# Attention, mixing and gated-MLP kernel on one core: the spatial product of three batches as seven half products

## Chip, cores and metric

The kernel runs on one core of a Trainium2 chip. The metric is the device time of one execution in microseconds (us). The times of before are 612.1, 614.9 and 610.61 us, median 612.1.

## The reference

Three models follow one another on B = 4 batches of S = 768 tokens with d = 384 features (8 heads of 48). First linear attention with a decayed state, then token mixing with a rotation by theta and a channel layer, then a gated MLP with a spatial product. Everything is float32.

```python
def _attn_ref(q, k, v, alpha):
    for t in range(S):
        state = alpha[:, :, t, :, None] * state + np.einsum('bhd,bhe->bhde', k[:, :, t], v[:, :, t])
        y[:, :, t] = np.einsum('bhd,bhde->bhe', q[:, :, t], state)

def _moe_ref(x, w_theta, w_tok_r, w_tok_i, w_ch):
    theta = x @ w_theta
    y = np.einsum('ts,bsd->btd', w_tok_r, x * cos(theta)) + np.einsum('ts,bsd->btd', w_tok_i, x * sin(theta))
    u = x + y
    return u + np.maximum(u @ w_ch, 0.0)

def _moe2_ref(x, w_in, w_spatial, b_spatial, w_out):
    h = np.maximum(x @ w_in, 0.0)
    u, v = h[..., :512], h[..., 512:]
    v_n = (v - mean(v)) / np.sqrt(var(v) + 1e-06)
    v_s = np.einsum('ts,bsd->btd', w_spatial, v_n) + b_spatial[None, :, None]
    return (u * v_s) @ w_out
```

The change concerns `v_s`: for each batch, the transpose of v_n (512 x 768) by the transpose of w_spatial (768 x 768).

## The kernel before

The kernel has three phases that overlap. The first (up to about 76 us) loads q, k, v, alpha and the weights of the mixing, in units of 128 tokens (`NU` = 24 units, 6 a batch), runs the decays as scans on DVE and the attention's small products on PE, and makes the first theta and z. The second is bound by the token mixing (`tokmix`, L731: 864 matmuls of 128x512 and 128x256), with the attention of later units and the channel layer (`ch_p`, L773) between them; it writes x of each batch to DRAM (`x2d`). The third, from about 420 us on, is the gated MLP.

All large products are made of float32r matmuls: each operand is held as a high part (a cast on ACT) and a low part (the difference, on DVE), and a product is three matmuls, high by high, high by low, low by high. "Split" below means such a cast with its difference.

The MLP goes batch by batch. With x split in two halves of 384 tokens (`x2_h` L843, `x2_l` L846), for each of six stripes s of 128 tokens:

- `v_p` (L857) makes v on PE: 9 matmuls of 128x512 into one of three PSUM buffers ("ps").
- `v_r` (L865, ACT) applies the ReLU into a "v" tile, of which there are two; `v_b` (L870 to L874, DVE) takes the statistics; `v_w` (L877, POOL) the power -1/2; `v_n` (L881, DVE) normalises; `v_h` (L888, ACT) and `v_l` (L892, DVE) split the result into `vns`.

Then come 8 tiles (f, h): 128 features f of four, 384 tokens h of two.

- `g_u` (L899) makes u on PE, 9 matmuls of 128x384, into the same three buffers; `g_r` (L907, ACT) applies the ReLU into "ur" (three tiles).
- `g_s` (L915) makes the spatial product: 18 matmuls of 128x384, six stripes by three, into one of five PSUM banks "acc".
- `g_m` (L924, L925, DVE) adds the bias and multiplies by u; `g_h` (L931, ACT) and `g_l` (L935, DVE) split the result into `gs`.

At last six stripes of the output: `o_p` (L944), 12 matmuls of 128x384 into "ps", `o_e` (L952, ACT) copies, `o_d` (L955) stores on SP's queue. `open_b` (L825) opens the pool of the MLP and loads the bias.

The order of instructions on each engine is worked out at build time. Each piece is a `step` with an engine, an estimated cost, predecessors (`after`), the buffers it takes (`tiles`) and a due time; `order` (L111) runs a small model of the engines and queues over the steps and always takes the ready step with the lowest number. That number is a latest start, worked out backwards, plus an offset of the step's kind from the tables `OFF`, `OFF0` (units of batch 0), `OFF3`, `UNIT` and `PIECE`. `LAG`, `AHEAD` and the costs of the loads are the planner's figures for transfers. SP's queue carries the loads of data and the stores, POOL's queue the first weights.

Of the kernel before, what the change touches and what calls it, by code (L numbers as in the profile page):

```python
# [30 lines left out]
DM = H * D  # L31
# [11 lines left out]
T0 = 512  # L43
OFF = {
# [27 lines left out]
}  # L72
OFF3 = {
# [18 lines left out]
STP = ()  # L92
NQ = 16
# [14 lines left out]
AHEAD = {"dma": 0.8, "queue": 1.0}  # L108
# [184 lines left out]
def attention_mixer_kernel(  # L293
# [67 lines left out]
    LAG = {"pe": 0.2, "dve": 0.14, "act": 0.15, "pool": 0.07, "dma": 0.6, "none": 0.0, "queue": 0.6}  # L361
# [71 lines left out]
    def conv(src, part, key, tiles=(), scale=None):  # L433
# [12 lines left out]
        if src.dtype == I64:  # L446
            c["queue"] = nc.gpsimd if n < NQ else nc.sync
            k = step(early + OFF["raw"], "queue" if n < NQ else "dma", 2.2 * size, raw_f64, n, after=before, tiles=[raw])
            k = step(early + OFF["mag"], "act", cost(0.54, 0.86), top, n, after=[k], tiles=[raw, zero])
            k = step(early + OFF["mul"], "dve*", cost(0.47, 0.87), join, n, after=[k], tiles=[raw, zero, f])  # L450
        else:
            k = step(early + OFF["raw"], "dma", 1.3 * size, raw_f32, n, after=before, tiles=[raw])
            f = raw
# [69 lines left out]
    def att_a(u):  # L523
# [284 lines left out]

    w2 = []
# [26 lines left out]

    def x2_load(b):
        x2[b] = p2.tile([128, KD, S], F32, tag="xT", name="x2", bufs=2)
        nc.sync.dma_start(x2[b], x2d[b])

    def x2_h(b, h):
        xq[b, h] = mpa[0].tile([128, 2, KD, TH], F32R, tag="xs2", name="xs2", bufs=3)
        nc.scalar.copy(out=xq[b, h][:, 0], in_=x2[b][:, :, h * TH:(h + 1) * TH])  # L843
# [285 lines left out]
    for h in range(2):  # L1129
        x2_split(0, h)  # L1130
# [104 lines left out]
```

## Time and profile before

| | us |
|---|---|
| median of three runs | 612.1 (610.61 to 614.9) |
| profiled execution | 610.03 |
| its span | 608.3 |
| PE busy in the span | 578.7 (95%) |
| DVE busy | 397.3 (65%) |
| ACT busy | 242.7 (40%) |
| POOL busy | 25.1 (4%) |
| mean granted clock of PE, share of full speed | 0.994 |
| moved by DMA | 63.77 MB |

The rows in the section further down come from this one execution. Busy times are sums of the durations of instructions; on PE neighbouring matmuls overlap, so distances from start to start are used where the length of a piece of work counts.

### The profile page before, as it was taken

The page shows a single profiled execution, that of the slowest core. Times are in us where ns is not written, and L with a number is a line of the kernel's source. Part 1 is how long each engine was busy: PE and PEld are TensorE (multiplying, and loading weights), DVE is VectorE, ACT ScalarE, POOL GpSimd, SP SyncE. Part 2 cuts the span into 40 slices and gives each one's busy share as a digit, 9 for nine tenths or more (in the row PEclk, how much of TensorE's full clock was granted, in tenths as well). Part 3 has the DMA queues.
Part 4 walks back from the last instruction along what each step waited for, and adds up shares of the span by engine and source line. Part 5 has one row for each costly group of instructions (what it writes and reads, how often), then busy time and mean ns, then how long its engine had stood idle before and what let it go on. Part 6 is the DMA issues. An engine that isn't in the chain of part 4 may idle for free.

```text
span 608.3 us, 13440 instructions
## 1 busy us (share of the span) xinstructions
PE 578.7 (95%) x5803; PEld 526.3 (87%) x5803; DVE 397.3 (65%) x668; ACT 242.7 (40%) x445; POOL 25.1 (4%) x45
## 2 busy tenths in 40 slices
PE   1778999999999999999999999999999999999997
PEld 1667778888988788888998899999999999999997
DVE  7798999987878878679467775535345633553330
ACT  3566656433352443345345533324223422242222
POOL 1100100000000000000000011001000100010000
PEclk9988999999999999999999999999999999999999
DMA  8856666532443244421027650201000110011002
GB/s 310 298 162 222 218 222 210 188 116 83 160 122 115 74 139 128 147 92 48 11 94 239 214 182 1 79 0 53 26 1 2 39 40 1 0 38 42 0 1 78
DMA packets 27370, 63.77 MB, mean 105 GB/s; under 512 B 2992, under 2 KB 12720, under 8 KB 26800
## 3 DMA queue, kind: packets, MB, share of 16 engines
q1 hardware_dynamic: 25136, 51.13, 25.4%
q0 software_dynamic: 2176, 11.80, 5.6%
q8 instruction: 45, 0.74, 0.5%
q14 instruction: 13, 0.11, 0.1%
HBM read 50.33 MB, written 9.44 MB: 98 GB/s over the span
## 4 chain that ended last, share of the span: by engine, by line
PE 75%; DVE 10%; DMA 8%; issue 4%; ACT 2%; SPq 1%; DVEq 0%; ACTq 0%; POOLq 0%
PE acc L731 17%; PE sp L915 17%; PE psv L857 8%; PE pu L899 8%; PE po L944 8%; PE psc L773 6%; DMA qk<-in_qk 4%; PE psy L612 3%; PE th L664 3%; PE th L667 1%; DVE qk L518 1%; PE psu L572 1%; DMA al<-in_al 1%; PE psa L532 1%; DVE wf L409 1%
## 5 line engine op out<-in xcount | busy, mean ns | idle before, releaser
L731 PE MATMUL acc<-w,zs 128*128 128x512 f32 (+1 forms) x864 | 174.1, 347 | 1.5 <-DVE xT L745 0.8
L731 PEld LDWEIGHTS acc<-w,zs 128*128 128x128 f32 x864 | 134.6, 190 | 20.2 <-DVE xT L745 1.3
L915 PE MATMUL sp<-w,vns 128*128 128x384 f32 x576 | 106.9, 338 | 0.0
L915 PEld LDWEIGHTS sp<-w,vns 128*128 128x128 f32 x576 | 102.0, 188 | 0.8
L899 PE MATMUL pu<-xs,w 128*128 128x384 f32 x288 | 55.1, 336 | 0.0
L944 PE MATMUL po<-w,gs 128*128 128x384 f32 x288 | 53.8, 338 | 0.4 <-ACT v L865 0.4
L857 PE MATMUL psv<-w,xs 128*128 128x512 f32 x216 | 53.9, 395 | 0.0
L931 ACT CAST gs<-t 128x384 fp32r<-128x384 f32 x32 | 16.5, 514 | 92.9 <-DVE t L925 88.1
L944 PEld LDWEIGHTS po<-w,gs 128*128 128x128 f32 x288 | 50.9, 188 | 1.4 <-ACT v L865 0.7
L899 PEld LDWEIGHTS pu<-xs,w 128*128 128x128 f32 x288 | 50.5, 188 | 0.4
L924 DVE TENSOR_TENSOR t<-sp,bsb 128x384 f32<-128x384 f32 x32 | 17.8, 558 | 49.9 <-PE sp L915 49.8
L857 PEld LDWEIGHTS psv<-w,xs 128*128 128x128 f32 x216 | 40.2, 188 | 7.8
L773 PE MATMUL psc<-us,wch 128*128 128x384 f32 (+1 forms) x243 | 41.4, 321 | 0.0
L773 PEld LDWEIGHTS psc<-us,wch 128*128 128x128 f32 x243 | 37.8, 189 | 0.6 <-DVE xT L783 0.2
L506 DVE TENSOR_TENSOR_SCAN al<-al,heads 112x536 f32<-112x536 f32 x24 | 30.5, 1270 | 10.2 <-DMA al<-in_al 10.2
L877 POOL TENSOR_TENSOR rs<-rs,mhalf 128x1 f32<-128x1 f32 x24 | 15.1, 629 | 444.5 <-DMA raw<-in_w_out 255.9
L664 PE MATMUL th<-wth,xh 128*128 128x384 f32 x144 | 30.9, 351 | 0.9 <-ACT x L620 0.9
L510 DVE TENSOR_TENSOR_SCAN al<-al,heads 112x536 f32<-112x536 f32 x24 | 30.6, 1275 | 0.8
L518 DVE TENSOR_TENSOR qk<-qk,al 112x1024 f32<-112x1024 f32 x24 | 29.2, 1218 | 2.8 <-DMA qk<-in_qk 2.5
L870 DVE BATCH_NORM_STATS2 stt<-v 128x6 f32<-128x512 f32 x24 | 16.6, 690 | 21.4 <-ACT v L865 21.2
L704 ACT CAST zs<-z 128x768 fp32r<-128x768 f32 x24 | 20.0, 834 | 24.0 <-DVE z L700 13.1
L935 DVE TENSOR_TENSOR gs<-t,gs 128x384 fp32r<-128x384 f32 x32 | 17.9, 558 | 17.7 <-ACT gs L931 17.7
(89 smaller groups left out, 793.1 us busy)
## 6 DMA issues: line engine op xcount, KB each, us to landing
qk<-in_qk SPq DMA_DIRECT2D x24, 512.0 KB, 5.1
vd<-in_v SPq DMA_DIRECT2D x24, 288.0 KB, 3.4
al<-in_al SPq DMA_DIRECT2D x24, 268.0 KB, 2.7
raw<-in_w_ti POOLq DMA_DIRECT2D x6, 768.0 KB, 5.9
raw<-in_w_tr POOLq DMA_DIRECT2D x6, 768.0 KB, 5.8
x<-x2d SPq DMA_DIRECT2D x4, 1152.0 KB, 5.1
out<-o SPq DMA_DIRECT2D x24, 192.0 KB, 1.9
x2d<-xT SPq DMA_DIRECT2D x6, 576.0 KB, 3.3
```

Source lines behind the costliest of these rows:

```text
L506: nc.vector.tensor_tensor_scan(out=back[:, ::-1], data0=line[:, ::-1], data1=one[:, ::-1], initial=1.0, op0=ALU.mult, op1=ALU.add)
L510: nc.vector.tensor_tensor_scan(out=line, data0=line, data1=one, initial=0.0, op0=ALU.mult, op1=ALU.add)
L518: nc.vector.tensor_tensor(out=x, in0=x, in1=st[u]["ar"], op=ALU.mult)
L612: nc.tensor.matmul(psy[par][64 * c:64 * c + 64, a, :], w, v, start=part == 0 or first, stop=part == 1,)
L664: nc.tensor.matmul(th, xh[:, 0, k], wth[:, pr, k], start=(k == 0 and pr == 0), stop=False)
L704: nc.scalar.copy(out=st[u]["zs"][:, 0], in_=st[u]["z"])
L731: nc.tensor.matmul(acc[b, n][:, c0:c1], zs[:, pl, ri, m * 128:(m + 1) * 128], w[:, pr, t0:t1], start=first and n != 1, stop=last, skip_gro ...
L773: nc.tensor.matmul(ps, wch[:, pl, k, m * 128:(m + 1) * 128], us[:, pr, k], start=(n == 0), stop=(n == 3 * KD - 1),)
L857: nc.tensor.matmul(ps, xs2[:, pl, k, o:o + 128], win[pr, "v"][:, k], start=(n == 0), stop=(n == 3 * KD - 1),)
L899: nc.tensor.matmul(pu, win[f // 2][:, pl, k * 256 + f % 2 * 128:k * 256 + f % 2 * 128 + 128], xq[b, h][:, pr, k], start=(n == 0), stop=(n ...
L915: nc.tensor.matmul(sp[:, :TH], vns[b, s][:, pl, f * 128:(f + 1) * 128], wsp[s][:, pr, t], start=(n == 0), stop=(n == 3 * NS - 1),)
L944: nc.tensor.matmul(po, gs[b][:, pl, f, s * 128:(s + 1) * 128], wo[f // 2][:, pr, f % 2 * DM:(f % 2 + 1) * DM], start=(n == 0), stop=(n == ...
```

## The change

For batches 1 to 3 the spatial product is taken as a product of 2 x 2 blocks. The left matrix is cut by features (0 to 255, 256 to 511) and by stripes (0 to 2, 3 to 5), the right one by stripes and by output tokens (`TH` = 384). Seven products of blocks, with sums and differences of blocks as operands, take the place of eight. Each is made for two groups c of 128 features; such a half product (`g_p`) is 9 matmuls of 128x384. Three PSUM banks serve one c; products 2, 7 and 4, 3 are added into the bank of 1, 6 and 5, and DVE reads a bank between products where its sum so far is used twice (`g_a`, `g_2`, `g_3`). The order for each c is product 1, 6, u, 2, 7, u, 4, u, 5, u, 3.

Stripes s and s + 3 are made as a pair (`V_ORDER`); the pair is mixed in place in the two "v" tiles (`s_mix`). Each pair is split in two unmixed and two mixed parts. The sums of weights (`t_mix`, `t_h`, `t_l`) are made once, in batch 0, from three loads of pairs of stripes (768 KB each); after batch 0's last spatial tile, the first three stripes' second halves in `wsp` are overwritten by a difference (`pair_h`, `pair_l`). Batch 0 keeps `g_s`.

```diff
-AHEAD = {"dma": 0.8, "queue": 1.0}
+AHEAD = {"dma": 0.9, "queue": 1.1}
+PRODUCT_BANK = {1: 0, 2: 0, 6: 1, 7: 1, 4: 1, 5: 2, 3: 2}
+V_ORDER = (0, 3, 1, 4, 2, 5)
...
-    LAG = {"pe": 0.2, "dve": 0.14, "act": 0.15, "pool": 0.07, "dma": 0.6, "none": 0.0, "queue": 0.6}
+    LAG = {"pe": 0.2, "dve": 0.14, "act": 0.15, "pool": 0.07, "dma": 0.9, "none": 0.0, "queue": 0.9}
...
+    def pair_h(j):
+        nc.scalar.copy(out=wsp[j][:, 0, TH:], in_=pairs[j][:, 0, :TH])
...
+    def t_mix(j):
...
+        for o, x, y in ((b11, b12, b11), (b12, b22, b12), (b22, b22, b11), (b21, b21, b22)):
+            nc.vector.tensor_tensor(out=o, in0=x, in1=y, op=ALU.subtract)
...
+    def x2_part(b, h):
+        x2[b, h] = wide_tile((KD, TH), F32, "x2")
+        nc.sync.dma_start(x2[b, h], x2d[b, :, :, h * TH:(h + 1) * TH])
...
-        xq[b, h] = mpa[0].tile([128, 2, KD, TH], F32R, tag="xs2", name="xs2", bufs=3)
+        xq[b, h] = mpa[0].tile([128, 2, KD, TH], F32R, tag="xs2", name="xs2", bufs=2)
...
+    def s_mix(b, j):
+        (a11, a21), (a12, a22) = ((s2["v", b, s][:, :FH], s2["v", b, s][:, FH:]) for s in (j, j + NJ))
+        nc.vector.tensor_tensor(out=a22, in0=a21, in1=a22, op=ALU.add)
+        for o, x, y in ((a21, a11, a21), (a11, a22, a11), (a12, a12, a11)):
+            nc.vector.tensor_tensor(out=o, in0=x, in1=y, op=ALU.subtract)
...
+    def s_part(b, j, n):
+        v = s2["v", b, j + NJ * n]
+        return (ms[b, j][:, :, FH:], v) if n else (ms[b, j][:, :, :FH], v[:, :FH])
...
+    def left(b, n, j, pl, c):
+        store, o = {1: (ms, 0), 3: (ms, FH), 5: (ms, 2 * FH), 2: (vns, 0), 4: (vns, FH), 6: (vns, 0), 7: (vns, FH)}[n]
...
+    def g_p(b, c, n):
+        x = PRODUCT_BANK[n]
...
+        for j in range(NJ):
+            for pl, pr in ((0, 0), (0, 1), (1, 0)):
+                nc.tensor.matmul(
+                    g, left(b, n, j, pl, c), right(n, j, pr),
+                    start=(n in (1, 5, 6) and i == 0), stop=(i == 3 * NJ - 1), skip_group_check=n not in (1, 5, 6),
+                )
+                i += 1
...
+    def g_a(b, c):
+        x = s2["g", b, c, 0]
+        for h in range(2):
+            nc.vector.tensor_tensor(out=slot(h), in0=x, in1=bsb[0][:, h * TH:(h + 1) * TH], op=ALU.add)
...
-        kal = at("al", "dma", 0.78, load_al, tiles=[al])
-        kqk = at("qk", "dma", 1.48, load_qk, tiles=[qk])
+        kal = at("al", "dma", 0.85, load_al, tiles=[al])
+        kqk = at("qk", "dma", 1.6, load_qk, tiles=[qk])
...
+                km = step(OFF["vm"], "dve*", 1.4, s_mix, b, j, after=[k2, ("s_l", b, j, 0)], tiles=[v, u], by=t + 10.4)
...
+        k1 = product(1)
+        ga = step(OFF["g_r"], "dve", 1.04, g_a, b, c, after=[k1], tiles=[bank(0), sm, p0, p1], by=t)
+        k6 = product(6)
...
+                    step(OFF["x2"], "dma", 1.9, x2_part, b + 1, h,
+                         after=[("ch_d", b + 1, q) for q in range(ch_n(b + 1))] + [("g_p", b, 1, n) for n in (3, 5, 6)],
+                         tiles=[("raw", RAWB, ("x2", b + 1, h))], by=t - 4.0)
```

Besides, x of batches 2 and 3 is loaded in two halves of 576 KB into the weights' raw buffers after the last products that use these; "xs2" has two tiles in place of three; batch 0 has two "ur" slots in place of three tiles; the output tiles lie in the former "zeros" tile. Costs of the other loads rise as those shown (v 0.84 to 0.92, weights 2.2 to 2.4 and 1.3 to 1.4, the copy of the mask product 0.35 to 0.45). Every value of `OFF`, `OFF0`, `OFF3`, `UNIT` and `PIECE` is new, so the order of all 24 units changes too.

The order on PE where the last spatial products of a batch end and those of the next begin. `sp` is a spatial tile, `psv` v, `po` an output stripe, `pu` u, `xs_n` a half of x; before, at the passage from batch 1 to batch 2:

```order
L857 MATMUL psv<-w,xs_5096 128x512 x9
L915 MATMUL sp<-w,vns 128x384 x18
L857 MATMUL psv<-w,xs_5096 128x512 x9
L915 MATMUL sp<-w,vns 128x384 x18
L944 MATMUL po<-w,gs 128x384 x12
L857 MATMUL psv<-w,xs_5612 128x512 x9
L944 MATMUL po<-w,gs 128x384 x12
L857 MATMUL psv<-w,xs_5612 128x512 x9
L944 MATMUL po<-w,gs 128x384 x12
L899 MATMUL pu<-xs_5096,w 128x384 x9
L944 MATMUL po<-w,gs 128x384 x12
L899 MATMUL pu<-xs_5612,w 128x384 x9
```

After, at the same passage (`acc<-w,mx` and `acc<-w,vns` are half products):

```order
L918 MATMUL psv<-w,xs_5717 128x512 x9
L1117 MATMUL po<-w,gs 128x384 x12
L918 MATMUL psv<-w,xs_5735 128x512 x9
L1117 MATMUL po<-w,gs 128x384 x24
L918 MATMUL psv<-w,xs_5717 128x512 x9
L918 MATMUL psv<-w,xs_5735 128x512 x18
L1117 MATMUL po<-w,gs 128x384 x12
L918 MATMUL psv<-w,xs_5717 128x512 x9
L991 MATMUL pu<-xs_5717,w 128x384 x18
L991 MATMUL pu<-xs_5735,w 128x384 x18
L1059 MATMUL acc_6006<-w,mx 128x384 x9
L1059 MATMUL acc_6018<-w,mx 128x384 x9
```

The v products of the next batch stood between the last spatial tiles and the outputs; now all stand behind the last half product, and four u stand in one piece ahead of the first half product.

DVE's instructions for the v stripes, one stripe before:

```order
L870 BN_STATS stt<-v 128x6
L872 BN_AGGR mv<-stt 128x2
L874 TENSOR_SCALAR rs<-mv 128x1
L881 TENSOR_SCALAR v<-v,mv,rs 128x512
L892 TENSOR_TENSOR vns<-v,vns 128x512
```

A pair of stripes after, in the same batch:

```order
L934 BN_STATS stt<-v 128x6
L936 BN_AGGR mv<-stt 128x2
L938 TENSOR_SCALAR rs<-mv 128x1
L945 TENSOR_SCALAR v<-v,mv,rs 128x512 x2
L984 TENSOR_TENSOR mx<-v,mx 128x256
L956 TENSOR_TENSOR vns<-v,vns 128x512
L968 TENSOR_TENSOR v<-v 128x256
L970 TENSOR_TENSOR v<-v 128x256 x3
L956 TENSOR_TENSOR vns<-v,vns 128x512
L984 TENSOR_TENSOR mx<-v,mx 128x512
```

Statistics and normalising are as they were, for two stripes; the four 128x256 operations of `s_mix` (L968, L970) and the splits of the unmixed and mixed parts (L984 and the second L956) are new.

The first loads on POOL's queue, where `raw` is the buffer of a weight on its way, before:

```order
L397 DMA raw<-in_w_ti 128x3072
L397 DMA raw<-in_w_theta 128x1536
L397 DMA raw<-in_w_theta 128x2x1536
L397 DMA raw<-in_w_tr 128x3072
L397 DMA raw<-in_w_ti 128x3072 x3
```

After:

```order
L405 DMA raw<-in_w_ti 128x3072
L405 DMA raw<-in_w_theta 128x1536
L405 DMA raw<-in_w_tr 128x3072
L405 DMA raw<-in_w_theta 128x2x1536
L405 DMA raw<-in_w_ti 128x3072
```

The second part of w_theta has changed places with the first w_tr. On SP's queue the first loads were al, al, v, constants, q and k; they are now al, q and k, v, constants, al.

## Rows read from the trace of the kernel before

**Rows 1.** Page: busy time of each engine, and the chain that ended last, by engine

```profile
PE 578.7 (95%) x5803; PEld 526.3 (87%) x5803; DVE 397.3 (65%) x668; ACT 242.7 (40%) x445; POOL 25.1 (4%) x45
...
PE 75%; DVE 10%; DMA 8%; issue 4%; ACT 2%; SPq 1%; DVEq 0%; ACTq 0%; POOLq 0%
```

**Rows 2.** Busy by stretch: us; PE, PEld, DVE, ACT, POOL; PE clock; DMA; GB/s

```profile
0.00:76.00 76.00, 53.96 (x844) 45.26 (x845) 65.01 (x102) 42.78 (x73) 8.96 (x19) 0.96 0.71 242
76.00:420.00 344.00, 340.18 (x3949) 301.99 (x3948) 258.53 (x426) 147.74 (x273) 8.43 (x13) 1.00 0.36 119
420.00:608.30 188.30, 184.60 (x1014) 179.00 (x1012) 73.76 (x142) 52.22 (x99) 7.74 (x13) 1.00 0.07 24
```

**Rows 3.** Costliest groups: line, operation, count; busy us, mean ns; idle before

```profile
L915 PE MATMUL sp<-w,vns 128*128 128x384 f32 x576 | 106.9, 338 | 0.0
```

**Rows 4.** Timeline 489 to 503 us: start, us, engine, line, [idle before <- releaser]

```profile
489.72 2.25 PE L857 MATMUL psv<-w,xs 128*128 128x512 f32 x9
...
491.81 2.25 PE L944 MATMUL po<-w,gs 128*128 128x384 f32 x12
492.01 0.60 ACT L865 ACTIVATE v<-psv 128x512 f32<-128x512 f32 x1 [1.57 <-PE psv L857]
492.64 0.70 DVE L870 BATCH_NORM_STATS2 stt<-v 128x6 f32<-128x512 f32 x1 [7.74 <-ACT v L865]
...
494.47 0.55 DVE L881 TENSOR_SCALAR v<-v,mv,rs 128x512 f32<-128x512 f32 x1 [0.73 <-POOL rs L877]
495.06 0.62 ACT L888 CAST vns<-v 128x512 fp32r<-128x512 f32 x1 [0.44 <-DVE v L881]
...
495.71 0.69 DVE L892 TENSOR_TENSOR vns<-v,vns 128x512 fp32r<-128x512 f32 x1 [0.69 <-ACT vns L888]
...
497.56 3.33 PE L915 MATMUL sp<-w,vns 128*128 128x384 f32 x18
...
500.72 1.72 PE L899 MATMUL pu<-xs,w 128*128 128x384 f32 x9
500.92 0.56 DVE L924 TENSOR_TENSOR t<-sp,bsb 128x384 f32<-128x384 f32 x1 [0.16 <-PE sp L915]
...
502.28 3.34 PE L915 MATMUL sp<-w,vns 128*128 128x384 f32 x18
```

**Rows 5.** Smaller DVE and ACT operations: group by form, then the timeline

```profile
L540 DVE TENSOR_TENSOR ax<-psa,cst_sb 128x256 f32<-128x256 f32 x21 | 8.7, 416 | 2.1 <-PE psa L532 2.1
...
391.42 1.15 ACT L843 CAST xs<-x 128x1152 fp32r<-128x1152 f32 x1
...
392.60 1.36 DVE L846 TENSOR_TENSOR xs<-x,xs 128x1152 fp32r<-128x1152 f32 x1 [0.49 <-ACT xs L843]
```

**Rows 6.** DMA issues: queue, count, KB each, median us from issue to landing

```profile
x<-x2d SPq DMA_DIRECT2D x4, 1152.0 KB, 5.1
...
x2d<-xT SPq DMA_DIRECT2D x6, 576.0 KB, 3.3
```

**Rows 7.** The start: longest wait of PE, busy by stretch, timeline

```profile
PE acc L556 <- DVE qk L518: 12.4, 1, 12.4
...
0.00:40.91 40.91, 21.81 (x379) 18.34 (x380) 33.79 (x55) 19.91 (x34) 5.56 (x13) 0.97 0.74 258
40.01:76.00 35.99, 33.05 (x472) 27.72 (x469) 32.12 (x50) 23.77 (x42) 3.94 (x7) 0.93 0.66 218
36.00:38.20 2.20, 0.10 (x1) 0.10 (x2) 2.20 (x4) 0.52 (x1) 0.00 (x0) 1.00 0.03 6
38.20:41.70 3.50, 3.50 (x41) 2.91 (x42) 3.50 (x6) 2.75 (x4) 0.53 (x1) 0.51 0.13 12
46.00:48.40 2.40, 0.70 (x9) 0.34 (x7) 1.60 (x3) 1.84 (x4) 0.00 (x0) 1.00 0.94 312
...
39.96 0.95 DVE L708 TENSOR_TENSOR zs<-z,zs 128x768 fp32r<-128x768 f32 x1
40.01 2.05 PE L731 MATMUL acc<-w,zs 128*128 128x512 f32 x6
```

More of the change, by code (lines that the diff above doesn't have):

```diff
@@ L92 @@
 STP = ()
+STILL = ()
 NQ = 16
@@ L447, in conv @@
             c["queue"] = nc.gpsimd if n < NQ else nc.sync
-            k = step(early + OFF["raw"], "queue" if n < NQ else "dma", 2.2 * size, raw_f64, n, after=before, tiles=[raw])
+            k = step(early + OFF["raw"], "queue" if n < NQ else "dma", 2.4 * size, raw_f64, n, after=before, tiles=[raw])
             k = step(early + OFF["mag"], "act", cost(0.54, 0.86), top, n, after=[k], tiles=[raw, zero])
@@ L451, in conv @@
         else:
-            k = step(early + OFF["raw"], "dma", 1.3 * size, raw_f32, n, after=before, tiles=[raw])
+            k = step(early + OFF["raw"], "dma", 1.4 * size, raw_f32, n, after=before, tiles=[raw])
             f = raw
@@ L861, in v_p, with v_first @@
                 n += 1
+    def v_first(b, s):
+        return (V_ORDER if b else range(NS)).index(s) < VNA
     def v_r(b, s):
@@ new lines, in attention_mixer_kernel, with g_t, g_2 @@
+    t1s = [None]
+    def g_t(b, f, h):
+        if t1s[0] is None:
+            t1s[0] = wst.tile([128, CW], F32, tag="f", name="t1", bufs=FB).rearrange("p (n t) -> p n t", n=2)
+        t = s2["t1", b, f, h] = t1s[0][:, take("t1", (b, f, h))]
+        return t
+    def g_a(b, c):
+        x = s2["g", b, c, 0]
+        for h in range(2):
+            nc.vector.tensor_tensor(out=slot(h), in0=x, in1=bsb[0][:, h * TH:(h + 1) * TH], op=ALU.add)
+    def g_2(b, c):
+        nc.vector.tensor_tensor(out=slot(2), in0=s2["g", b, c, 1], in1=slot(1), op=ALU.add)
@@ L1118, in v_all @@
         k = step(OFF["vm"], "dve*", 0.46, v_n, b, s, after=[k], tiles=[v], by=t + 8.4)
-        k = step(OFF["vh"], "act", 0.53, v_h, b, s, after=[k, kb if s >= VNA else None, chain.get("v")], tiles=[v, vn], by=t + 9.0)
-        step(OFF["vl"], "dve*", 0.6, v_l, b, s, after=[k], tiles=[v, vn], by=t + 9.7)
+        kn[b, s] = k
+        if not b or i:
+            k = step(OFF["vh"], "act", 0.53, v_h, b, s, after=[k, None if low else kb, chain.get("v")], tiles=[v, vn], by=t + 9.0)
+            k2 = step(OFF["vl"], "dve*", 0.6, v_l, b, s, after=[k], tiles=[v, vn], by=t + 9.7)
@@ new lines, in plain @@
+    def plain(b):
+        nonlocal t
+        fh = [(f, h) for f in range(KF) for h in range(2)]
+        for n in range(len(fh) + LEAD):
+            if n < len(fh):
+                gate(b, *fh[n])
+            if n >= LEAD:
+                f, h = fh[n - LEAD]
+                bank = (f"acc{(2 * f + h) % 5}", 1, ("g", b, f, h))
+                k = step(
+                    OFF["g_s"], "pe", 3.12, g_s, b, f, h, by=t,
+                    after=[("v_l", b, s) for s in range(NS)] + [k for s in range(NS) for k in ready("wsp", s)]
+                    + [chain.get("s")],
+                    tiles=[bank] + [vn_tile[b, s] for s in range(NS)] + [("w", 12, ("wsp", s)) for s in range(NS)],
+                )
+                chain["s"] = k
+                t += 3.12
+                k = step(OFF["g_m"], "dve", 0.48, g_b, b, f, h, after=[k, klb], tiles=[bank, ("t1", 2, (b, f, h)), ("f", FB, "t1")], by=t + 0.5)
+                close(b, f, h, k)
@@ L1129, in attention_mixer_kernel @@
+    kn = {}
     for h in range(2):
@@ L1167, in attention_mixer_kernel @@
+        if b + 1 < B:
+            for s in V_ORDER:
+                tv = v_all(tv, b + 1, s)
         for s in range(NS):
-            if b + 1 < B:
-                t = v_all(t, b + 1, s)
             ps, o = ("ps", 3, ("o", b, s)), ("o", 2, (b, s))
             k = step(
-                OFF["o_p"], "pe", 2.09, o_p, b, s, by=t,
-                after=[("g_l", b, f, s // 3) for f in range(KF)] + [k for j in range(2) for k in ready("wo", j)]
-                + [chain.get("o")],
-                tiles=[gs_t, ps] + [("w", 12, ("wo", j)) for j in range(2)],
+                OFF["o_p"], "pe", 2.09, o_p, b, s, by=t + (12.9 if s >= NS - late else 0.0),
+                after=[("g_l", b, f, s // 3) for f in range(KF)] + [k for j in range(2) for k in ready("wo", j)],
+                tiles=[("gs", 1, b), ps] + [("w", 12, ("wo", j)) for j in range(2)],
```

309 lines of the change are left out of this document (243 added, 66 removed), and 36 rows, old and new, of tables (OFF, OFF0, OFF3).

## Prediction

> **What bounds the kernel now.** I read the busy times first: PE is busy 578.7 of 608.3 us, and the chain of work that ended last runs over PE for 75% of the span [rows 1]. The table by stretches then shows where PE's 29.6 idle us lie [rows 2]: 76.0 - 54.0 = 22.0 us before 76 us, 3.8 us from there to 420 us, and 188.3 - 184.6 = 3.7 us in the last stretch, all of it behind the last matmul. So the stage that the change touches, from 420 us on, is a PE stage without a gap, and DVE, at 73.8 us of 188.3, has room there. In such a stage a matmul less is time less, as long as nothing new makes PE wait.
>
> **What the seven products remove.** The spatial product is 576 matmuls of 128x384, 144 a batch [rows 3]. One tile of 18 goes from 497.56 to 500.72 us, 3.16 us (durations overlap, so I take start to start), hence 1.58 us for the nine matmuls of a half product [rows 4]. A batch has 8 tiles, 16 half products; batches 1 to 3 now do 14. That is 6 half products less: 6 x 1.58 = **9.5 us**. (The Trainium skill, "TensorE: Matmul & The Clock Gate", Back-to-back issue gap, gives columns over 2.4 GHz plus 2.5 ns for a matmul. By that 384 columns are 162.5 ns, an estimate, and the 54 matmuls would bring 8.8 us. The row has 176 ns, and it decides.)
>
> **What they add.** For each pair of stripes (s and s+3) DVE gets a mixing step of four 128x256 operations, a third split of 128x512 and one of 128x256; each batch gets eight more 128x384 operations, the reads of PSUM between products. Prices: 0.69 us for 128x512 and 0.56 us for 128x384 [rows 4]. For 128x256 no such row exists; bounds are zero and 0.56 us, and I take 0.42 us, that of a DVE operation of this size [rows 5]. A pair thus costs 7.3 us of DVE in place of 4.5, and a batch 3 x 2.8 + 8 x 0.59 = 13 us more. With 24 operations of 128x384 for the weights' sums in batch 0 (13.4 us), DVE rises from 74 to about 126 of 180 us. It does not become the bound on average. What counts is the order in which each engine must do it.
>
> **The boundary between batches 1 and 2.** Now PE does the next batch's v products under the previous spatial products, and each has 4.6 us from PE's end to its split (491.81 to 496.40 us) [rows 4]. After the change a stripe needs its partner, there are two v buffers, and a pair must be mixed and split before the next pair's ReLU can write them. PE has cover in the new order: u, o, u, o, v, o, v, o, o, v, v, v, o, v, four u, then product 1. Take t = 0 at the end of the last product. With 1.56 us for u (500.72 to 502.28), 2.11 for o (12 matmuls at 0.176) and 2.09 for v (489.72 to 491.81) [rows 4], the second v of pair 0 ends at 13.6. Behind it, with 0.20 us from PE to ACT, and 0.03 to 0.05 from one of ACT and DVE to the other and between DVE operations: ReLU to 14.4, statistics and power to 16.3 (1.83 us from 492.64 to 494.47), normalise to 16.8, high to 17.5, low to 18.2, mixing (4 x 0.42 and gaps) to 20.0, v's second high and low to 21.4, the mixed part's to 22.1 [rows 4]. Pair 1's ReLUs wait for these buffers: 21.45 and 22.2; its mixing ends at 28.8, its last split at 30.9. Pair 2's first ReLU runs from 30.2 to 30.8, and only then frees its PSUM buffer, of which there are three. PE comes to the second u, which takes this buffer, at 29.9, and waits until 30.9: 1.0 us. Product 1 then starts at 35.75 instead of 34.55, so **1.2 us** in all. Product 6 needs the last low part, at 39.4, and PE reaches it at 40.5. Inside the products PE waits once: product 7 of the second half needs DVE's sum at 53.3, and PE is there at 53.1; **0.3 us** with the hop. So 1.5 us at this boundary, and the same 1.5 at the next, whose order differs only ahead of the first v.
>
> At the first boundary the v products are earlier (x is loaded early), but nothing may be split into the shared buffers before the three stripes of weights are overwritten, which waits for the last spatial tile of batch 0. Counted the same way from there, the first quarter of the last pair is split at 22.1 and PE is at product 1 at 21.0: **1.1 us**.
>
> x of batches 2 and 3 now comes in halves after the last product. No row has this load; its bounds are nothing and 5.1 us, that of a load of twice the size, and I take 3.3 us, a transfer of the same size [rows 6]. With 0.6 us to issue and the split's 1.15 on ACT and 1.36 on DVE [rows 5] the first half is ready at 6.4, and v starts at 7.3: hidden under u, o, u, o. At 5.1 us it would cost 0.9.
>
> In batch 0 the sums of weights stand ahead of DVE's reads of the first spatial tiles. Five banks cover those, but the gate's buffers are now two, and the sixth u waits for the third's ReLU: about **0.6 us** (bounds zero and one spatial tile, 3.2). The three loads of weights for it, 768 KB each, land while PE does its last v and u products.
>
> **The new order of the first 420 us.** All offsets are new, and the planner counts transfers as slower. The place that can pay is the start. PE's first matmul waits 12.4 us for DVE's product on the first q and k [rows 7]; the first q and k now stand second on SP's queue, behind one load of al instead of two, v and the constants, so PE starts earlier. But on POOL's queue the second part of w_theta, which the first theta product needs, now stands behind a w_tr load. The split of the first z ends on DVE at 40.9 us (39.96 + 0.95); DVE has been busy for 33.8 us by then and has waited 7.1 [rows 7]. The token mixing starts 0.9 us before that end, at 40.0. In the new order DVE has 2.0 us more of instructions ahead of this point (each at the mean of its kind); I give the waits 1.0 us more, since the second theta weight comes later. The first token mixing is then at 43.0 us, 3.0 later. PE has by then done 1.6 us more (instructions that now stand behind), so it has idled 1.4 us more. Behind this point PE now idles 36.0 - 33.05 = 2.9 us up to 76 us, and its clock fell to half, 1.2 GHz, behind the gap of 36 to 38.2 us and stayed there for 3.5 us, a loss of 3.5 x 0.49 = 1.7 us; the gap of 46 to 48.4 us is followed by another such stretch (its row reads alike) [rows 7]. The new order has token mixing in longer stretches there, so I let 1.2 of the 2.9 us and one of the two half-clock stretches go: 1.4 - 1.2 - 1.7 = **-1.5 us**. Bounds: a loss of 6.8 us (3.0 late, nothing regained, and one more gap with half clock behind it, 2.1 + 1.7) and a gain of 7.2 us (both gaps, 2.1 and 1.7, and both half-clock stretches gone).
>
> **Sum.** The profiled execution took 610.0 us, 608.3 its span and 1.7 around it. 610.0 - 9.5 + 1.1 + 1.5 + 1.5 + 0.6 - 1.5 = 603.7 us. The median of the three timed runs, 612.1, lies 2.1 above the profiled execution, and the runs lie 0.6 to 4.9 above it; I add 1.1, so **604.8 us**.
>
> **Rivals.** (a) *The waits are hidden and the whole 9.5 us arrives.* For it: the waits are of about 1 us each, the size of my errors over ten steps. Against: the pairs hang on two buffers, which no order removes. 610.0 - 9.5 - 1.5 + 1.1 = 600.1 us, less if the start gains more.
> (b) *The pair chain eats the saving.* Each pair 1 us longer, or the x halves at 5.1 us, makes each boundary 3 us dearer: 604.8 + 3 x 2.5 = 612.3, no change. For it: DVE, ACT and POOL take turns in one chain, and any instruction of another step ahead of them in a queue is added to it. [...] (The Trainium skill, same page, Architectural detail, says that ACT and DVE take their instructions strictly in order, which speaks against a change that gives both more of them; no row here tells it from the program's own order.)
> (c) *Slower: the start.* The theta weight behind w_tr delays the first mixing, and nothing regains it: 6.8 us lost for 1.5 gained is 604.8 + 8.3 = 613.1 us. It is slower than before from a loss of 5.8 us on; by over 1% from 11.9 us on. For it: by 40 us the queues are in one another's way already. Against: PE starts earlier, and the holes of now are themselves no small part of 76 us.
>
> **How the numbers follow.** Forecast (601 to 608.5): 0.45. Whole gain (below 601): 0.22. Eaten (608.5 to 613): 0.20. Start (above): 0.13. The range leaves out a third of the second and half of the last: **599 to 612.5**; the forecast's own is 601 to 608.5. One per cent, about what this kernel's timing can tell, is 606.0 and 618.2: faster takes all of the second and two thirds of the first, 0.52; slower half of the last, 0.07; the rest 0.41.
>
> **What would show it.** In the profile after: spatial matmuls 522 instead of 576; PE from the first v of batch 2 to that of batch 3 about 61 us for 63 now; PE's waits for the ReLU of v at the fourth-last u, some 1 us, three waits of 1 to 1.5 us a batch at most; no wait of v for x; the first token mixing near 43 us. I am wrong if PE's idle time from 420 us on (less the tail's 3.7) is near zero or over 8 us, or if idle time and half clock before 76 us differ from now by over 4 us.

## The result and the profile after

The changed kernel takes 605.87 us (median of 8 runs, 604.73 to 609.87) where the kernel before takes 612.09 us (8 runs beside it): ratio 0.9915, 95% interval 0.9887 to 0.9943, so 5.2 us less (3.5 to 6.9; the two medians lie 6.2 apart). Forecast were 604.8 us. The sum came out nearly right, but by luck: two of its terms were wrong by 4 to 6 us each, in opposite directions.

The profiled execution took 607.0 us, its span 605.2. The page's busy times and the chain that ended last by engine, and the busy time by stretch (columns as in [rows 2]):

```profile
PE 570.2 (94%) x5749; PEld 516.9 (85%) x5749; DVE 443.0 (73%) x770; ACT 256.6 (42%) x475; POOL 25.9 (4%) x45
...
PE 74%; DVE 10%; ACT 3%; issue 2%; DMA 2%; POOL 0%; ACTq 0%; DVEq 0%; POOLq 0%
```

```profile
0.00:76.00 76.00, 49.09 (x793) 40.93 (x794) 66.38 (x104) 41.53 (x68) 10.01 (x21) 0.96 0.73 254
76.00:420.00 344.00, 339.55 (x3969) 301.42 (x3967) 264.37 (x438) 150.94 (x286) 6.13 (x8) 1.00 0.35 116
420.00:605.20 185.20, 181.56 (x991) 174.57 (x989) 112.28 (x230) 64.15 (x122) 9.78 (x16) 1.00 0.10 37
```

Against [rows 1] and [rows 2]: PE's busy time falls by 578.7 - 570.2 = 8.5 us. PE's idle time before 76 us rises from 22.0 to 26.9 us, from there to 420 us from 3.8 to 4.5, and in the last stretch it stays (3.7 before, 3.6 now). So -8.5 + 4.9 + 0.7 - 0.1 = -3.0, and the spans differ by 3.1. The products bring about what they should, the tail takes little of it back, and in this execution the start gives up more than half of it.

The spatial products now stand in four groups: 144 plain matmuls in batch 0 (L1030) and 378 in half products (L1059, two groups of 162 shown and one of 54), 522 in all where [rows 3] has 576 (page, columns as there).

```profile
L1059 PE MATMUL acc<-wt,vns 128*128 128x384 f32 x162 | 30.7, 337 | 0.0
L1059 PE MATMUL acc<-w,mx 128*128 128x384 f32 x162 | 30.6, 338 | 0.0
```

The gain can be read from start to start too. Half products stand 1.58 us apart, as counted (last two rows). From the first v of batch 2 (472.75 us, shown below) to that of batch 3 (first row) PE takes 60.3 us:

```profile
533.02 2.25 PE L918 MATMUL psv<-w,xs 128*128 128x512 f32 x9
...
565.40 1.74 PE L1059 MATMUL acc<-wt,vns 128*128 128x384 f32 x9
566.98 1.74 PE L1059 MATMUL acc<-w,mx 128*128 128x384 f32 x9
```

In the kernel before the same two points are 63.1 us apart:

```profile
461.30 2.26 PE L857 MATMUL psv<-w,xs 128*128 128x512 f32 x9
...
524.39 2.26 PE L857 MATMUL psv<-w,xs 128*128 128x512 f32 x9
```

A batch is thus 2.8 us shorter: two half products, 3.16 us, less some 0.4 us that PE loses at the passage.

### The profile page after: what moved, and what is told of

Same layout as the page of the kernel before. It is cut to its first block, busy times and chain, and to the rows that moved or that the text cites. A ratio compares the mean times of both kernels' runs of the same rounds, so it can differ in the third digit from the quotient of the medians.

```text
span 605.2 us, 13522 instructions
## 1 busy us (share of the span) xinstructions
PE 570.2 (94%) x5749; PEld 516.9 (85%) x5749; DVE 443.0 (73%) x770; ACT 256.6 (42%) x475; POOL 25.9 (4%) x45
## 4 chain that ended last, share of the span: by engine, by line
PE 74%; DVE 10%; ACT 3%; issue 2%; DMA 2%; POOL 0%; ACTq 0%; DVEq 0%; POOLq 0%
PE acc L739 21%; PE acc L1059 11%; PE pu L991 8%; PE po L1117 6%; PE psc L781 6%; PE psv L918 6%; PE sp L1030 4%; PE th L672 3%; PE psy L620 2%; PE psa L540 2%; PE th L675 2%; DMA al<-in_al 2%; PE psu L580 1%; DVE al L514 1%; PE psk L564 1%
## 5 line engine op out<-in xcount | busy, mean ns | idle before, releaser
L739 PE MATMUL acc<-w,zs 128*128 128x512 f32 (+1 forms) x864 | 174.9, 347 | 2.3 <-DVE acc L748 1.2
L739 PEld LDWEIGHTS acc<-w,zs 128*128 128x128 f32 x864 | 134.7, 190 | 20.1 <-DVE xT L753 1.5
L991 PE MATMUL pu<-xs,w 128*128 128x384 f32 x288 | 53.3, 337 | 0.4 <-ACT v L929 0.4
L1059 PE MATMUL acc<-wt,vns 128*128 128x384 f32 x162 | 30.7, 337 | 0.0
L1059 PE MATMUL acc<-w,mx 128*128 128x384 f32 x162 | 30.6, 338 | 0.0
L411 ACT ACTIVATE zeros<-raw 128x768 f16<-128x768 bf16 (+1 forms) x22 | 22.8, 1038 | 17.3 <-DMA raw<-in_w_ti 7.7
L526 DVE TENSOR_TENSOR qk<-qk,al 112x1024 f32<-112x1024 f32 x24 | 29.2, 1217 | 0.0
L679 ACT ACTIVATE kk<-th,magic 128x384 f32<-128x384 f32 x24 | 13.9, 579 | 35.7 <-PE th L675 35.6
L716 DVE TENSOR_TENSOR zs<-z,zs 128x768 fp32r<-128x768 f32 x24 | 22.9, 954 | 8.2 <-ACT zs L712 8.2
```

What stands on the lines that cost most here:

```text
L526: nc.vector.tensor_tensor(out=x, in0=x, in1=st[u]["ar"], op=ALU.mult)
L716: nc.vector.tensor_tensor(out=zs[:, 1], in0=st[u]["z"], in1=zs[:, 0].bitcast(F32), op=ALU.subtract)
L739: nc.tensor.matmul(acc[b, n][:, c0:c1], zs[:, pl, ri, m * 128:(m + 1) * 128], w[:, pr, t0:t1], start=first and n != 1, stop=last, skip_gro ...
L991: nc.tensor.matmul(pu, win[f // 2][:, pl, k * 256 + f % 2 * 128:k * 256 + f % 2 * 128 + 128], xq[b, h][:, pr, k], start=(n == 0), stop=(n ...
L1059: nc.tensor.matmul(g, left(b, n, j, pl, c), right(n, j, pr), start=(n in (1, 5, 6) and i == 0), stop=(i == 3 * NJ - 1), skip_group_check=n ...
```

## The passages between batches

All waits of PE from 400 us on, and then the passage from batch 1 to batch 2 in the timeline (columns as in [rows 4]; the products of batch 1 end at 465.36 us):

```profile
PE pu L991 <- ACT v L929: 0.4, 2, 0.2
```

```profile
472.57 1.35 DVE L909 TENSOR_TENSOR xs<-x,xs 128x1152 fp32r<-128x1152 f32 x1
472.75 2.26 PE L918 MATMUL psv<-w,xs 128*128 128x512 f32 x9
...
486.47 0.60 ACT L929 ACTIVATE v<-psv 128x512 f32<-128x512 f32 x1 [0.30 <-DVE vns L956]
...
492.62 1.34 DVE L970 TENSOR_TENSOR v<-v 128x256 f32<-128x256 f32 x3
493.54 0.62 ACT L952 CAST vns<-v 128x512 fp32r<-128x512 f32 x1 [1.29 <-DVE v L970]
493.66 1.73 PE L991 MATMUL pu<-xs,w 128*128 128x384 f32 x9
...
494.93 0.60 ACT L929 ACTIVATE v<-psv 128x512 f32<-128x512 f32 x1 [0.24 <-DVE vns L956]
...
495.58 4.96 PE L991 MATMUL pu<-xs,w 128*128 128x384 f32 x27 [0.18 <-ACT v L929]
...
500.38 3.32 PE L1059 MATMUL acc<-w,mx 128*128 128x384 f32 x18
```

PE's order is the planner's: two half products on mixed parts, then product 2, and only then 6, where the change was told as 1, 6, u, 2. The wait is at the place that was forecast, the second u of the last four, and for the forecast cause, the ReLU of the third pair's v that must free its PSUM buffer. It is 0.18 us long where 1.0 was forecast; from start to start the second u comes 0.36 us later than 1.56 us behind the first (493.66 to 495.58). Counted from 465.36, the times forecast and measured are: first v 7.3 and 7.4; pair 1's first ReLU 21.45 and 21.1; its mixing's end 28.8 and 28.6; pair 2's first ReLU 30.2 and 29.6; PE at the second u 29.9 and 29.9 (493.66 + 1.56); product 1 35.75 and 35.0. Most of the error is one overlap in each pair that I had not counted: ACT's cast of the mixed stripe starts at 493.54, 0.4 us before the last of the three mixing operations ends at 493.96.

At the passage from batch 0 to batch 1 nothing waits:

```profile
432.97 0.42 DVE L984 TENSOR_TENSOR mx<-v,mx 128x256 fp32r<-128x256 f32 x1
...
433.85 3.33 PE L1059 MATMUL acc<-w,mx 128*128 128x384 f32 x18
```

PE reaches product 1 at 21.0 us behind the last spatial tile, as forecast (412.81 to 433.85). The first part of the last pair is split at 433.39, 20.6 us behind it, not 22.1.

## The start

PE's three largest waits in the changed kernel before 76 us (for what, us in total, times, longest), and then the first token mixing:

```profile
PE acc L540 <- DVE qk L526: 11.6, 3, 7.7
PE pst L640 <- ACT x L628: 5.3, 3, 2.5
PE acc L580 <- ACT kt L568: 3.3, 2, 2.7
```

```profile
42.84 2.27 PE L739 MATMUL acc<-w,zs 128*128 128x512 f32 x6
```

PE's longest wait for DVE's product on q and k is 7.7 us (11.6 in three) instead of the 12.4 of [rows 7], and the first token mixing comes at 42.84 us (forecast 43.0). Up to here the forecast held. But behind it PE idles more, not less, and this is where 6 us of the forecast were lost:

```profile
40.00:76.00 36.00, 26.79 (x363) 22.23 (x355) 33.42 (x50) 23.37 (x38) 4.99 (x9) 0.91 0.72 245
```

From 40 to 76 us PE idles 9.2 us, 7.1 of them behind 42.84 us; the kernel before idled 2.9 us behind its first token mixing [rows 7]. Up to the first mixing idle time rose by 0.8 us, where 1.4 was forecast. There are two half-clock stretches, 42 to 45.5 and 69.5 to 73 us (granted clock 0.52 and 0.55), as there were two before. The token mixing done by 76 us shows it too, before (L731) and after (L739), groups of the first 76 us:

```profile
L731 PE MATMUL acc<-w,zs 128*128 128x512 f32 (+1 forms) x97 | 22.1, 370 | 0.7 <-DVE w L429 0.4 <-DVE zs L708 0.3
```

```profile
L739 PE MATMUL acc<-w,zs 128*128 128x512 f32 (+1 forms) x72 | 16.2, 377 | 0.0
```

DVE is busy for 66.4 us of these 76 in the changed kernel and for 65.0 in the one before: it does no less, but in another order.

## Experiments

**Theories.** A: the seven products bring their 9 us whole, and the new order of the start loses 3 to 5 us of it. B, its rival: the tail brings only some 5 to 6 us, and the start's loss belongs to the one profiled execution. To part them, orders were crossed. In these kernels the planner's call is replaced by a fixed list; `listed` emits the steps in the list's order as soon as their predecessors and buffers allow it:

```diff
-        for key in order(latest(steps, due)):
+        for key in listed(steps, SEQUENCE):
             runs[key](*key[1:])
```

**Old start, new tail.** SEQUENCE is the kernel before's list up to the end of the token mixing, with the changed kernel's tail.

> The seven products and their order behind the token mixing as in the changed kernel; every instruction up to the end of the token mixing in the order that the kernel before had on each engine. Theory A (the tail brings all of its 9.5 us, and the new order of the start gives 3 to 5 us of that back): 612.1 - 9.5 = 602.6 us, some 3.3 below the changed kernel, and PE idle before 76 us near 22 us instead of 26.9. Theory B (the tail brings only about 6 us; the start costs nothing on the median, and the profiled execution was an unlucky one): 605.9 us.

607.36 us, ratio 0.9907 (0.9881 to 0.9933): by the time alone, theory B. The profile says otherwise (first 76 us, and the seam):

```profile
0.00:76.00 76.00, 53.36 (x844) 44.34 (x845) 64.78 (x102) 43.02 (x73) 8.95 (x19) 0.96 0.72 240
...
340.00:400.00 60.00, 56.80 (x323) 52.14 (x322) 46.04 (x92) 25.58 (x44) 6.06 (x7) 1.00 0.27 95
```

The start idles 22.6 us, much as before, but 3.2 us are lost where the two lists meet; the changed kernel has no gap there:

```profile
340.00:400.00 60.00, 60.00 (x345) 55.47 (x344) 51.51 (x97) 28.32 (x49) 5.04 (x6) 1.00 0.41 139
```

The crossing brought a wait of its own, so this run does not decide.

**Old tail, new start.** The same the other way round.

> The kernel before, with the plain products, but with the changed kernel's order of all instructions up to the end of the token mixing. Theory A: 612.1 + 3 to 5 = 615 to 617 us. Theory B: 612 us.

623.46 us, ratio 1.0169 (1.0145 to 1.0192). Slower, as A says, but by far too much: 5.2 us are lost at the seam, and half clock in the start grew:

```profile
0.00:76.00 76.00, 52.73 (x807) 44.01 (x808) 67.61 (x106) 43.08 (x71) 10.01 (x21) 0.89 0.77 261
...
340.00:400.00 60.00, 54.81 (x312) 49.36 (x311) 40.08 (x74) 23.62 (x37) 3.86 (x7) 1.00 0.36 119
```

**Old first half.** The old order only up to some 190 us, where PE works without gaps.

> The changed kernel with the first half of its instructions (up to about 190 us; PE works without gaps there) put in the order of the kernel before, and the rest, with the end of the token mixing and the seven products, in the order of the changed kernel. Theory A (the new order loses 4 to 5 us before 76 us and the tail brings its whole 9.5): idle time and half clock by 120 us as before (47 us in place of 51.8), no new waits at 340 to 370 us, and 612.5 - 9.5 = 603 us, a ratio near 0.985. Theory B (the tail brings only 6 us): a ratio near 0.991 as the changed kernel has.

613.36 us, ratio 1.0011 (0.9983 to 1.0038): neither theory. The start is the old one again (22.6 us idle), but this seam loses even more. From 120 to 340 us PE idles 9.9 us, where it idles 2.1 in the kernel before and 4.0 in the changed one, and the clock falls (0.99 over the stretch):

```profile
120.00:340.00 220.00, 210.09 (x2819) 183.04 (x2818) 156.80 (x248) 85.30 (x170) 0.00 (x0) 0.99 0.32 100
```

**Old order up to batch 0's spatial products.** The seam is put behind the token mixing's end and among batch 0's MLP, and the changed kernel itself was run beside it.

> The changed kernel once more, unchanged, beside the next two on the same chip. Its ratio to the kernel before was 0.9915 (0.9887 to 0.9943); expected the same, 0.990 to 0.993, and by theory A idle time and half clock before 120 us near 30.7 us once more (26.9 in the kernel before), near nothing from 400 us to the last stores.

> The seven products behind the kernel before's order, with the seam placed later than in the first such run: all instructions up to the end of batch 0's spatial products, its v and u among them, stand in the order of the kernel before, and only what is new, and batches 1 to 3, in that of the changed kernel. Theory A: 26.9 us of idle time and half clock before 120 us, 3.5 from there to 340 us, and none of the 3.2 us of waits that the first seam cost at 347 to 368 us: 612.4 - 9.5 = 603 us, a ratio near 0.985. Theory B (the tail brings only some 6 us): 0.991.

The changed kernel: 606.84 us, ratio 0.991 (0.9872 to 0.9947), as the first time. The crossed one: 609.29 us, 0.9951 (0.9921 to 0.9981). Its seam costs 3.1 us in one wait, with half clock behind it (0.97 over the 60 us from 340 us on, 1.8 us more):

```profile
PE pu L991 <- ACT ur L1022: 3.1, 1, 3.1
```

```profile
376.42 1.34 ACT L850 CAST wt<-pair 128x384 fp32r<-128x384 f32 x3 [0.90 <-DVE pair L844]
...
377.37 2.33 DVE L844 TENSOR_TENSOR pair<-pair 128x384 f32<-128x384 f32 x4
...
380.25 0.49 ACT L1022 ACTIVATE ur<-pu 128x384 f32<-128x384 f32 x1 [2.49 <-DVE t L1096]
```

ACT's ReLU of u stands behind six casts of the weights' sums, and then waits 2.49 us for the product on DVE (L1096) that frees its "ur" slot and stands behind four subtractions of those sums (377.37). Meanwhile PE waits for the PSUM buffer that this ReLU frees. So the next run took batch 0's u products, their ReLUs and the spatial products in the changed kernel's order:

> As the run with the old order up to batch 0's spatial products, but with the u products, their ReLUs and the spatial products of batch 0 in the changed kernel's order (five u, three spatial tiles, then u again), so that no u waits behind the casts of the weights' sums. Theory A: the 3.1 us of wait and the 1.7 us of half clock at 340 to 400 us of that run are gone, and the ratio falls from 0.995 to 0.987: 604 us, below the changed kernel by 2 to 3 us on the median. If it stays at 0.991 or above, the old start is worth no more than the new one on the median, whatever single profiles show.

603.79 us (600.85 to 604.7), ratio 0.9857 (0.9832 to 0.9882): 8.7 us less than before (7.2 to 10.3), about 3.5 us below the changed kernel by the ratios. Theory A had 0.987. This version beats both kernels: its interval ends below that of the changed kernel (0.9887 to 0.9943). The first 76 us and the seam:

```profile
0.00:76.00 76.00, 57.16 (x843) 47.75 (x844) 65.06 (x102) 42.88 (x73) 8.96 (x19) 0.93 0.71 239
...
340.00:400.00 60.00, 58.88 (x336) 54.49 (x335) 47.23 (x95) 25.54 (x44) 5.01 (x7) 1.00 0.31 109
```

Idle time and half clock change places from one execution to the next: the changed kernel idles 26.9 us by 76 us at a clock of 0.96 in its first profile and 24.4 us at 0.93 in its second. So to compare starts over all runs, take PE's idle time by 76 us plus 76 us times what the clock lacks of 1 (the clock is given to two digits, so each value is good to 0.4 us). Old order: 25.1 in the kernel before, 25.7, 23.1, 25.7 and 24.2 in the four kernels with its start; mean 24.8. New order: 30.0 in the changed kernel, 29.8 in its second profile, 31.6 with the old tail, 28.7 and 28.5 in the two kernels below that change only the tail; mean 29.7. The order of the start costs 4.9 us by these profiles, each of one execution, and 3.5 us by the times of this version and of the changed kernel. B falls.

**What in the start?** Four edits sought one cause. In the changed kernel PE waits twice for ACT's copy of the attention rows, L628, with work of others ahead of it on ACT (timeline at 60 us; the attention products that it copies ended at 60.1):

```profile
60.27 0.84 ACT L712 CAST zs<-z 128x768 fp32r<-128x768 f32 x1 [0.45 <-DVE z L708]
...
61.41 0.84 ACT L429 ACTIVATE w<-wf 128x768 fp32r<-128x768 f32 x1 [0.30 <-DVE wf L417]
...
62.36 1.06 ACT L411 ACTIVATE zeros<-raw 128x768 f16<-128x768 bf16 x1
63.29 0.51 ACT L628 COPY x<-psy 128x192 f32<-128x192 f32 x2
...
63.86 0.55 PE L640 MATMUL pst<-cst_sb,x 128*128 128x128 f32 x3 [2.51 <-ACT x L628]
```

ACT waits 0.30 us for DVE while the copy behind it could run. (The Trainium skill, "TensorE: Matmul & The Clock Gate", Architectural detail, says that ACT and DVE take their instructions strictly in order; the trace agrees, in these rows and at the seam above, where ACT stands idle for 2.49 us.)

```diff
 CAST zs<-z 128x768
+COPY x<-psy 128x4x48 x2
 ACTIVATE w<-wf 128x768
 ACTIVATE zeros<-raw 128x768
-COPY x<-psy 128x4x48 x2
```

> The changed kernel with two moves in ACT's order at the start, nothing else: the copy of unit 2's attention rows stands ahead of the cast of z of unit 0 (it stood behind it), and that of unit 3 ahead of two steps of the weights' conversion (it stood behind them). Theory A1 (PE's waits of 2.2 us at 42 us and of 2.5 us at 64 us come from ACT's order): the second falls from 2.5 to about 0.4 us, the first to about 1.1 with the next piece starting 0.6 us earlier; 2 to 3 us in all, 603 to 604 us. Theory A2 (PE would wait anyway behind them, for DVE's scans and q, k): less than 1 us, 605 to 606.

608.62 us, ratio 0.9923 (0.9902 to 0.9944): no gain. The waits did fall (first row, of this kernel from 38 to 76 us; 4.7 us in two waits in the changed kernel there), but in this execution PE ran 7.5 us at about half clock where the first profile of the changed kernel has full clock with gaps (second row, this kernel):

```profile
PE pst L640 <- ACT x L628: 1.5, 1, 1.5
```

```profile
57.50:65.00 7.50, 7.50 (x112) 6.15 (x111) 6.64 (x11) 6.14 (x11) 0.61 (x2) 0.54 0.82 282
```

The changed kernel in the same stretch:

```profile
57.50:65.00 7.50, 4.91 (x112) 3.76 (x110) 6.63 (x11) 6.01 (x11) 0.77 (x2) 1.00 0.87 294
```

PE did 112 matmuls in both. By 76 us idle time and half clock together come to 30.0 us in both. That the clock fell because the waits were gone is not shown: the second profile of the changed kernel, with its waits in place, makes up that sum as this run does (24.4 us idle at a clock of 0.93; here 24.7 at 0.93).

Next, the load that rival (c) named:

```diff
-DMA raw<-in_w_tr 128x3072
 DMA raw<-in_w_theta 128x2x1536
+DMA raw<-in_w_tr 128x3072
```

> The changed kernel with the second part of w_theta and the first w_tr exchanged on POOL's queue and in their conversion, so that w_theta comes first as before. By the rival of the prediction that named this load as the cause of a late start: the first theta product, the first mixing (42.8 us) and all behind them come 2 to 3 us earlier, 603 us. If the load is not what the first theta product waits for (in the trace PE comes to it right behind a product of the attention): no change, 605.9 us.

608.44 us, ratio 0.9931 (0.9907 to 0.9955), and 28.4 us idle by 76 us. The first token mixing comes at 42.42 us, 0.4 us earlier and not 2 to 3. The load of w_theta is not the cause.

Then the conversions of w_ch, which the token mixing does not need:

```diff
-DMA raw<-in_w_ch 128x1536
...
-DMA raw<-in_w_ch 128x2x1536
...
 DMA raw<-in_w_tr 128x3072
+DMA raw<-in_w_ch 128x2x1536
+DMA raw<-in_w_ch 128x1536
```

> The changed kernel with the two loads of w_ch and their conversions (3.0 us of DVE and 3.0 of ACT before 76 us) moved behind the last weights of the token mixing, nothing else. Theory A2 (the start is bound by DVE's and ACT's work, and the new order puts weights that PE does not need yet ahead of the units that it needs): 2 to 4 us less by 76 us, 604 to 606 where the changed kernel has 607.8 on this chip (ratio 0.986 to 0.989). If DVE's and ACT's order is not the cause: ratio 0.991.

612.16 us, ratio 0.9999 (0.9976 to 1.0021): worse. The idle time by 76 us stays at 26.2 us (29.2 with half clock, where 2 to 4 us less were forecast), and a new wait appears at 105 us, again for the copy. On ACT it stands behind the moved conversions, which wait for DVE, and behind a later one that waits 1.35 us for the load of w_in:

```profile
104.45 0.84 ACT L429 ACTIVATE wch<-wf 128x768 fp32r<-128x768 f32 x1 [1.60 <-DVE wf L417]
```

```profile
110.34 0.90 PE L640 MATMUL pst<-cst_sb,x 128*128 128x128 f32 x3 [5.05 <-ACT x L628]
```

And all conversions of the first sixteen pieces at their old places among the units' instructions:

> The changed kernel with only the conversions of the first sixteen pieces of weights (their loads, high and low parts) put where the kernel before had them among the units' instructions; the units' own order stays new. If the place of these conversions makes the start slower: idle time and half clock before 120 us fall from 30.7 to about 27 us, ratio 0.986. If it is the order of the units' own instructions (scans, attention, theta): they stay at 30 us or more, ratio 0.991.

615.06 us, ratio 1.0049 (1.0025 to 1.0073): worse still, with much waiting for the same copy (7.6 us in four waits by 120 us). Idle time and half clock come to 32.1 us by 76 us and to 38.2 by 120 us, where 27 or 30 was forecast:

```profile
PE pst L640 <- ACT x L628: 7.6, 4, 3.9
```

So neither the load of w_theta, nor the two copies, nor the conversions of w_ch before 76 us are the cause by themselves. What the place of all conversions costs is not settled, since the last two runs brought waits of their own. The old order of the start is better as a whole; which of its differences does it stays open.

**Is the pair's chain really at its limit?** Since the forecast waits did not come, the chain was made longer.

```diff
             nc.vector.tensor_tensor(out=o, in0=x, in1=y, op=ALU.subtract)
+        for v in (s2["v", b, j], s2["v", b, j + NJ]):
+            nc.vector.tensor_scalar(out=v, in0=v, scalar1=0.0, scalar2=None, op0=ALU.add)
```

> The changed kernel with two more DVE operations of 128x512 (adding zero, 0.55 us each) behind the mixing of every pair of stripes: 1.2 us more a pair. Theory C (the pair's chain through the two v buffers is at its limit, so that PE waits only 0.2 us now): the second of the last four u products then waits 2.4 us more at the passages 1 to 2 and 2 to 3 (two pairs stand ahead of the third pair's ReLU), product 1 at the passage 0 to 1 about 2.1 us: 7 us more, 615, and more where the clock falls behind such a wait. Theory D (there is slack that I did not see): less than 1 us more.

613.2 us, ratio 1.0008 (0.9982 to 1.0034): 5.7 us slower than the changed kernel by the ratios. PE's waits from 400 us on, and one of the two long ones:

```profile
PE pu L993 <- ACT v L929: 3.8, 2, 1.9
PE acc L1061 <- DVE vns L956: 0.2, 1, 0.2
```

```profile
496.29 6.52 PE L993 MATMUL pu<-xs,w 128*128 128x384 f32 x27 [1.91 <-ACT v L929]
```

At the passages 1 to 2 and 2 to 3 the wait grew by 1.7 us each, and behind the first of them PE's clock was 0.79 in the 8 us from 496 us on, 1.7 us more; behind the second it stayed at 1.00. The pair grew by 0.9 us: the split of the mixed stripe now follows the mixing by 1.15 us (427.15 to 428.30) instead of 0.23 (427.84 to 428.07), and two pairs stand ahead, 2 x 0.9. So theory C holds there: nothing is left between the chain and PE. At the passage 0 to 1 it did not hold. PE started product 1 at 432.40 while the low part of the last pair was ready only at 433.60, and it did not wait. A product takes its three stripes one after another. The last stripe's high part, needed 1.05 us after the start, was ready at 432.72, and only the ninth matmul, 1.4 us after the start (8 x 0.176), takes the low part. PE waited 0.2 us a few products later, for another split.

**What are 54 more matmuls worth?** Product 2 of batches 1 to 3 left out (the output misses it):

```diff
-        for j in range(NJ):
+        for j in range(0 if n == 2 else NJ):
             for pl, pr in ((0, 0), (0, 1), (1, 0)):
```

> The changed kernel without product 2 of batches 1 to 3 (54 matmuls of 128x384 less, the output misses this part), everything else in place. If the tail is PE's alone, this brings what the change brought by its own 54 matmuls: 6 x 1.58 = 9.5 us less, 598.3 on this chip. If other engines hold the tail by now, it brings less and PE's waits on ACT and DVE grow.

600.32 us, ratio 0.9815 (0.9771 to 0.986): 6.1 us below the changed kernel by the ratios (some 3 either way by the two intervals), of 9.5. PE's busy time is 562.8 us, against 571.7 in the changed kernel's second profile with the same clock in the start, so 8.9 us went. But now PE waits in the tail for DVE's reads between products, beside the 0.4 us for v as before:

```profile
PE acc L1059 <- DVE small L1079: 2.4, 3, 0.9
```

A half product saved at this place is no longer worth its full time.

## The prediction, step by step

- **PE bounds the tail: right.** 0.4 us of waits from 400 us on beside the stores at the end.
- **Six half products, 9.5 us: right.** They start 1.58 us apart as counted, and a batch is 2.8 us shorter (3.16 less the passage). PE's busy time fell by 8.5 us (7.0 against the second profile); 54 matmuls left out took 8.9; the version with the old start gains 8.7 us (7.2 to 10.3). (The Trainium skill, "TensorE: Matmul & The Clock Gate", Back-to-back issue gap: by its formula for one matmul by itself the 54 bring 8.8 us, an estimate. The trace has 176 ns from start to start where the formula gives 162.5.)
- **The boundaries, +1.1, +1.5, +1.5: too dear.** 1 to 2 and 2 to 3: some 0.4 us each (product 1 at 35.0 for 34.55), by the overlap of split and mixing. The wait of 0.3 us at product 7 did not come, and of the 1.2 us forecast ahead of product 1 only 1.0 was a wait that the text accounts for. 0 to 1: nothing. The chain there was counted 1.5 us too long (20.6 for 22.1). In the run with the longer chain the part was ready 22.2 us behind the last spatial tile, and product 1 still did not wait: the step that failed was to count an operand as needed when a product starts.
- **x in halves, hidden: right.** Landing took 4.9 us where I took 3.3, near the upper bound of [rows 6], and v started at 7.4 us for 7.3: PE had outputs and u to do, and the second half's split at 472.57 us stands beside the first v.
- **Batch 0, +0.6: did not come;** PE is busy for 60.00 of the 60 us from 340 us on. A 128x256 operation takes some 0.42 us, as taken from [rows 5] (L970, three in 1.34 us with the gaps between them).
- **The start, -1.5: wrong,** with the wrong sign. The first mixing came when forecast, but "I let 1.2 of the 2.9 us and one of the two half-clock stretches go" has no row behind it, and this is the step that failed: behind the first mixing idle time rose by 4.1 us instead, and the mean clock stayed at 0.96. I had counted DVE's work ahead of the first mixing and none of the new order's waits behind it. The longest of those are for ACT's copy, but taking them away gained nothing, so the cause stays open. The loss, 4.9 us, lies within the bound of 6.8 that was kept for rival (c), which named the place, but its mechanism, the load of w_theta, was not it.
- **The rivals and the signs.** Of the tail rival (a) was right: its waits are hidden but for 0.4 us. Rival (b) says 3 us a boundary and adds 2.5 (with 3 it would be 613.8 us); its price was near, since 0.9 us more a pair cost 5.7 us in the run with the longer chain. Both signs by which the prediction called itself wrong are there: less the 3.7 us of the end, idle time from 420 us on is near zero, and idle time and half clock before 76 us differ by 4.9 us, over the 4 allowed. The time came as forecast, but only in part for the reasons given.
- **The sum:** with the measured terms it is 610.0 - 8.5 + 4.9 + 0.7 - 0.1 = 607.0, what the profiled execution took. Forecast were 603.7 for it, and 604.8 for the median, which is 605.87. It came near by luck: the tail was made 3.8 us too dear and the start 6.4 us too cheap, 0.7 us of idle time between 76 and 420 us was not forecast, and the first profiled execution lies 1.1 us above its median where the forecast has it 1.1 below.

## What to carry to other kernels

When a planner's order is made anew for a change in one stage, look at every other stage too: here the tail's gain was 8.7 us by the run with the old start, and the new start gave 3.5 of it back. A new tail can be had with the old order of the rest, if the place where the two meet is looked at row by row, since each seam can cost as much as the gain. On an engine that works in order, a step that waits for another engine makes everything behind it late, however ready it is; for a chain through two buffers, count each pair's excess once for every pair ahead, and an operand of an accumulation as needed when its own matmul comes, not when the product starts.

## What was not expected

Taking away 3.2 us of waits at 42 and 64 us gained nothing: in the profile PE ran at about half clock (0.54) from 57.5 to 65 us instead of idling 2.6 us of it. Idle time and half clock also trade places between two executions of one and the same kernel, so one profile of such a start says little about either alone. A DVE operation of 128x512 that adds a constant in place took 0.38 us (two in 0.76 us), less than the 0.55 us of the one with two per-partition operands in [rows 4] (row of the run with the longer chain):

```profile
427.19 0.76 DVE L972 TENSOR_SCALAR v<-v 128x512 f32<-128x512 f32 x2
```
